# A front reordered around a two-taps-a-product convolution, and one relu over two units, in a convolution with two mixture layers

## The chip, the core and the metric

The kernel runs on one core of one Trainium2 chip. The metric is the device time of one execution in microseconds (us); the median of several executions is compared. Five engines work side by side, each through its own queue of instructions: PE (TensorE, matrix products), ACT (ScalarE), DVE (VectorE), POOL (GpSimd) and SP (which here only issues DMAs).

## The reference

```python
def _attn_ref(x, weight):            # x: 2 x 4096 x 192, weight: 8 heads x 7 taps
    w = softmax(weight)              # over the 7 taps, with 1e-9 in the divisor
    out[t] = sum over k of w[head, k] * x_pad[t + k]      # causal, head by head of channels

def _moe_ref(x, w_in, w_out):        # x: 8192 x 192, w_in: 192 x 2048, w_out: 2048 x 192
    h = x @ w_in
    g = where(h >= 1, h, where(h <= -1, 0, (h + 1)**2 / 4))
    return g @ w_out

def _moe2_ref(x, w_in, w_out):
    h = x @ w_in
    return (h * sigmoid(1.702 * h)) @ w_out

# the result is _moe2_ref(_moe_ref(_attn_ref(x)))
```

## The kernel before, in words

The 8192 tokens are cut into 16 blocks of T = 512. The 192 channels are cut into an "a" part of 128 (one block to a tile) and a "b" part of 64 (two blocks to a tile). For each block the kernel makes the convolution and then two layers, numbered 1 (the clipped square) and 2 (the sigmoid product). Each value of x, of the weights and of the gate is split into a high and a low part (`xah`, `xal`; `ghi`, `glo`), and a product is made from three products of the parts.

**Units and steps.** A unit is one slice of 128 hidden channels of one layer and one block; there are 16 units for each of 32 phases (a phase is a layer and a block), 512 in all. The main loop takes two units a step. `both(u, v)` puts on PE the first product of units u, u+1 (into one of two `pair` tiles of two banks each, which alternate from step to step) and the second product of units u-4, u-3 (into the two `acc` banks of a phase). The products have 64 rows, and PE is given them in couples, the low half of the rows beside the high half, 19 couples a step. The `pair` tile is complete with the 15th couple.

**Gates.** `gates(u)` turns the two banks of a `pair` tile into `ghi` and `glo`. For layer 1: ACT makes relu((h+1)/2) into tile `a` (line 319) and its square (line 320), DVE takes the bound max(h, 1) and the smaller of it and the square (line 326), ACT makes the high part (line 330), DVE the low part (line 334). Three forms exist. In the first two phases (`units[u][0] < B`, with the conversions of weights in between, the "fill" below) relu and square run over both units at once. In the later layer 1 phases the four operations `early(0), bound(0), early(1), bound(1)` run unit by unit; these are 14 phases of 8 steps, 112 steps. In layer 2 it is one activation a unit (line 322), its high and its low part.

**Order.** Everything is written in program order inside `manual_schedule`; each engine takes its own instructions in that order and waits on semaphores. Beside the gates some steps hold other work, placed by `at(unit, op)`: the convolution of later blocks on DVE (lines 185, 186, two taps a step, some of them in layer 1 steps), its parts (lines 79, 80), the end of a phase (`finish`, lines 465 to 492). The weights come as 64 bit words through SP; `convert_at` sets the steps at which each tile of weights (two units of one layer) is loaded, scaled (ACT), shifted and joined (DVE), and split into high and low (line 155 on ACT or DVE, lines 160 and 165 on DVE).

**The front.** Before the loop: taps and x are loaded, PE runs two products on constants (`warm_up`), DVE and ACT make the exponentials of the taps, ACT makes seven diagonals of 128 by 128 for the b part of both blocks, POOL six for the a part of block 1. PE convolves the b part in quarters of its array (line 215, seven taps), DVE the a part of block 0 (lines 185, 186), and PE six taps of the a part of block 1 with 128 by 128 diagonals (line 204), two taps before the first products of units 0, 1 (`first_only(0)`) and four behind them; ACT makes the seventh tap (line 220). Then come `first_only(2)` and, as step 2, the first `both`. Step n below is the one with units 2n and 2n+1.

Of the kernel before, what the change touches and what calls it, by code (L numbers as in the profile page):

```python
# [8 lines left out]
F32 = mybir.dt.float32  # L9
# [6 lines left out]
P = 128  # L16
# [4 lines left out]
def kernel(  # L21
# [46 lines left out]
    def bank(n, name):  # L68
        return ps.tile([P, T], F32, tag=f"bank{n}", name=name)
# [5 lines left out]
    def f32(ap):  # L75
        return ap.bitcast(F32)
# [12 lines left out]
    def exponentials():  # L89
        mx = const.tile([P, 2], F32, name="mx")  # L90
        nc.vector.tensor_reduce(mx, taps, axis=AX.X, op=ALU.max)
        nc.vector.tensor_sub(taps, taps, mx.unsqueeze(2).to_broadcast([P, 2, K]))
        nc.scalar.activation(exps, taps, AF.Exp)

    def softmax_taps():
        return [
            lambda: nc.vector.tensor_reduce(share, exps, axis=AX.X, op=ALU.add),
            lambda: nc.vector.tensor_scalar_add(share, share, 1e-9),
            lambda: nc.vector.reciprocal(share, share),
            lambda: nc.vector.tensor_mul(taps, exps, share.unsqueeze(2).to_broadcast([P, 2, K])),  # L100
        ]


    words = {1: w1, 2: w2}
# [67 lines left out]
    def new_xs():  # L172
        return [xs_p.tile([P, T], F32R, tag=t, name=t) for t in ("xah", "xal", "xbh", "xbl")]

    def x_load(part, i, queue=None):

        t = xt_p.tile([P, T + 128], F32, tag=f"xt{part}", name="xt", bufs=2 - part)[:, 0 : PAD + T]
        (queue or nc.sync).dma_start(t, (xb if part else xa)[i])
        return t
# [7 lines left out]

        return [tap(k) for k in range(K)]

    def warm_up(w):  # L190
# [6 lines left out]
    def diagonals(part, eng_mul, d):  # L197
        for k in range(len(d)):
            eng_mul(d[k], ident, exps[:, part, k : k + 1])

    def conv_on_pe(t, c, d):

        def tap(k):
            return lambda: nc.tensor.matmul(c, d[k], t[:, k : k + T], start=False, stop=k == len(d) - 1)  # L204

        return [tap(k) for k in range(len(d))]

    def conv_by_quarters(t, cs, d):

# [6 lines left out]

        return [lambda k=k: tap(k) for k in range(K)]

    def first_tap(part, t, c, k):
        nc.scalar.mul(c, t[:, k : k + T], exps[:, part, k : k + 1])  # L220

    def high_of_sum(part, hi, c):
        nc.scalar.mul(hi, c, share[:, part : part + 1])
# [87 lines left out]
    def gate_ops(u):  # L311

        n, _ = phases[units[u][0]]
        h = hid.pop(u)
        a = a_p.tile([P, 2, T], F32, tag="a", name="a")

        def early(k=slice(0, 2)):
            if n == 1:
                nc.scalar.activation(a[:, k], h[:, k], AF.Relu, bias=0.5, scale=0.5)  # L319
                nc.scalar.activation(a[:, k], a[:, k], AF.Square)  # L320
            else:
                nc.scalar.activation(a[:, k], h[:, k], AF.Gelu_apprx_sigmoid)  # L322
# [12 lines left out]

        return early, bound, high, low

    def gates(u, conversions=()):
        early, bound, high, low = gate_ops(u)
        if units[u][0] < B:  # L340
            early()
            for op in conversions:
# [163 lines left out]


    def gates_beside_finish(u, p, conversions):
        early, bound, high, low = gate_ops(u)
        up, down, add, bh, bl, ah, al = finish_ops(p)  # L510
        ops = [early, up, ah, down, *conversions, lambda: bound(0), lambda: bound(1), al, add]
# [31 lines left out]
    def fetch_x(*which):  # L543
        for part, i in which:
            xt[part, i] = x_load(part, i)
# [11 lines left out]
    with tc.manual_schedule():  # L557
        first, second = halves_of
        nc.sync.dma_start(taps, taps_in)
        xt[1, 0] = x_load(1, 0, nc.scalar)  # L560
        xt[0, 0] = x_load(0, 0)
        xt[0, 1] = x_load(0, 1, nc.scalar)
        fetch_w(1, 0, first)
        fetch_w(1, 1, first)
        fetch_w(1, 0, second)
        fetch_w(1, 1, second)
# [4 lines left out]
        exponentials()  # L571
# [6 lines left out]
        shares = softmax_taps()  # L578
        db = o_p.tile([P, K, P], F32, tag="o", name="diag")
        db = [db[:, k] for k in range(K)]  # L580
        da = [f32(t).rearrange("p (k c) -> p k c", c=P) for t in new_xs()]
        da = [da[k // 4][:, k % 4] for k in range(K - 1)]
        diagonals(1, nc.scalar.mul, db)
        diagonals(0, nc.gpsimd.tensor_scalar_mul, da)
        b_ops = conv_by_quarters(xt[1, 0], cb_ps, db)
        a1 = conv_on_pe(xt[0, 1], ca_ps, da)
# [15 lines left out]
        steps += ((5, 7, 8, 9, 9, 10), (6, 8, 10, 11, 11, 12), (8, 10, 12, 13, 13, 14), (9, 11, 14, 15, 15, 16))  # L602
# [9 lines left out]
        def of(ops, step):  # L612
            return ops.get(step, [])

        w0, w1_ = parts_of(0), parts_of(1)
        run(*b_ops)
        run(lambda: nc.scalar.activation(table, ident[:, 0:1], AF.Gelu_apprx_sigmoid))
        run(*a0[0:5], *shares, *w0[0][0:2], lambda: first_tap(0, xt[0, 1], ca_ps, K - 1), *w0[0][2:4])
        run(*a0[5:], *w0[0][4:], w1_[0][0], *put_sum(0, 0), *w1_[0][1:3], *put_sum(0, 1), *w1_[0][3:])
        straight, crossed, last, closing = first_only(0)  # L620
        run(*a1[0:2], straight, last, lambda: crossed(closing), *a1[2:])
        run(*of(fetches, 0))
        run(*w0[1], *put_sum(1, 1), *w1_[1][0:3])
        early, bound, high, low = gate_ops(0)
        run(*of(act, 0))
        early()
        run(*of(dve, 0))
        bound(0)
        run(*put_sum(1, 0))
        bound(1)  # L630
        for k in (0, 1):
            high(k)
            low(k)
        run(*w1_[1][3:])
        straight, crossed, last, closing = first_only(2)
        run(straight, last, lambda: crossed(closing))
        run(*of(fetches, 1), *of(dve, 1))
        gates(2, of(act, 1))

        def beside(step):  # L640
            for op in plan.get(step, []):
# [77 lines left out]
```

## Time and profile before

| what | value |
|---|---|
| runs | 1179.79, 1181.0, 1181.41 us; median 1181.0 |
| the profiled execution's own time | 1180.55 us |
| its span (first to last instruction) | 1178.8 us |
| PE matmul, busy | 1150.7 us |
| PE weight load, busy | 924.6 us |
| ACT, busy | 841.1 us |
| DVE, busy | 718.0 us |
| POOL, busy | 5.5 us |
| DMA, mean | 26 GB/s |

An execution takes 1.75 us more than its span here. Busy time counts the stretches in which at least one instruction of the engine was running. A row of a timeline is: start, duration, engine, line, operation, tiles, shape, and in brackets the idle time of the engine ahead of it with what ended it; a count xN at the end says that N equal instructions that follow each other are merged.

### The profile page before, as it was taken

To read this page: it belongs to the slowest core of one execution; us is meant where nothing else is said; L and a number is where in the kernel's file an instruction comes from. 1 tells how busy PE (TensorE), PEld (TensorE's weight loads), DVE (VectorE), ACT (ScalarE), POOL (GpSimd) and SP (SyncE) were. 2 spreads that over 40 slices of the span, in tenths; PEclk is the share of its full clock that TensorE was granted. 3 is DMA by queue.
4 is the path that set the end of the run, shared out by engine and by line. 5 is a ranking of instruction groups with operands and counts; after the bars stand their busy time and mean duration, and the time that the engine had idled before them with its cause. 6 is when DMAs were issued, how large, how long until landed. Compare 5 with 4: busy or idle time off the path is not lost.

```text
span 1178.8 us, 23909 instructions
## 1 busy us (share of the span) xinstructions
PE 1150.7 (98%) x9780; PEld 924.6 (78%) x9780; DVE 718.0 (61%) x1099; ACT 841.1 (71%) x1420; POOL 5.5 (0%) x12
## 2 busy tenths in 40 slices
PE   9999999999999999999999999999999999999998
PEld 4999986677786877868778787787878778787786
DVE  7997756675646756466574655646556475564533
ACT  7998677776767677676776667767677676776754
POOL 1000000000000000000000000000000000000000
PEclk9999999999999999999999999999999999999999
DMA  6442011000100001000010000100001000000000
GB/s 187 120 119 60 1 44 30 1 10 14 28 11 14 11 14 28 11 14 10 15 37 1 15 10 15 37 13 3 10 15 37 15 1 10 14 11 14 2 1 28
DMA packets 23756, 30.44 MB, mean 26 GB/s; under 512 B 3296, under 2 KB 15840, under 8 KB 23648
## 3 DMA queue, kind: packets, MB, share of 16 engines
q1 hardware_dynamic: 23216, 28.27, 8.4%
q8 instruction: 77, 1.26, 0.4%
q10 hardware_dynamic: 432, 0.66, 0.2%
q14 instruction: 31, 0.25, 0.1%
HBM read 18.96 MB, written 6.29 MB: 21 GB/s over the span
## 4 chain that ended last, share of the span: by engine, by line
PE 66%; ACT 20%; DVE 11%; issue 3%; DMA 0%; ACTq 0%; DVEq 0%
PE acc L417 33%; PE pair L417 31%; DVE a L326 10%; ACT a L320 8%; ACT a L319 7%; ACT ghi L330 3%; DVE glo L334 1%; PE cb_ps L215 1%; ACT o L488 1%; DVE cva L186 1%; ACT o L492 0%; PE ca_ps L204 0%; PE acc L391 0%; DMA taps<-in_taps_dram 0%; DVE cva L185 0%
## 5 line engine op out<-in xcount | busy, mean ns | idle before, releaser
L417 PE MATMUL acc<-ghi,wt 64*128 64x512 f32 x3048 | 666.9, 388 | 0.0
L417 PE MATMUL acc<-glo,wt 64*128 64x512 f32 x2032 | 574.2, 389 | 0.0
L417 PEld LDWEIGHTS acc<-ghi,wt 64*128 64x128 f32 x3048 | 465.1, 184 | 54.3
L334 DVE TENSOR_TENSOR glo<-a,ghi 128x512 fp32r<-128x512 f32 x512 | 351.1, 689 | 203.6 <-ACT ghi L330 185.6
L417 PE MATMUL pair<-xah,wt 64*128 64x512 f32 x2048 | 444.5, 397 | 22.4 <-DVE a L326 22.3
L417 PEld LDWEIGHTS acc<-glo,wt 64*128 64x128 f32 x2032 | 329.2, 184 | 51.1 <-DVE glo L334 18.2
L330 ACT CAST ghi<-a 128x512 fp32r<-128x512 f32 x512 | 315.7, 618 | 45.7 <-DVE a L326 35.5
L417 PEld LDWEIGHTS pair<-xah,wt 64*128 64x128 f32 x2048 | 278.8, 184 | 85.0 <-DVE a L326 56.2
L326 DVE SCALAR_TENSOR_TENSOR a<-pair,a 128x512 f32<-128x512 f32 x256 | 175.5, 690 | 229.2 <-ACT a L320 229.2
L417 PE MATMUL pair<-xal,wt 64*128 64x512 f32 x1024 | 298.6, 387 | 0.0
L417 PE MATMUL pair<-xbh,wt 64*128 64x512 f32 x1024 | 274.5, 387 | 0.0
L322 ACT ACTIVATE a<-pair 128x512 f32<-128x512 f32 x256 | 152.1, 594 | 124.1 <-PE pair L417 124.1
L319 ACT ACTIVATE a<-pair 128x512 f32<-128x512 f32 (+1 forms) x240 | 150.0, 625 | 121.4 <-DVE a L326 96.0
L417 PEld LDWEIGHTS pair<-xbh,wt 64*128 64x128 f32 x1024 | 187.8, 184 | 18.5
L417 PE MATMUL pair<-xbl,wt 64*128 64x512 f32 x512 | 197.3, 387 | 0.0
L320 ACT ACTIVATE a<-a 128x512 f32<-128x512 f32 (+1 forms) x240 | 158.6, 661 | 7.6
L417 PEld LDWEIGHTS pair<-xal,wt 64*128 64x128 f32 x1024 | 142.9, 184 | 18.8
L417 PEld LDWEIGHTS pair<-xbl,wt 64*128 64x128 f32 x512 | 93.9, 184 | 9.0
L186 DVE SCALAR_TENSOR_TENSOR cva<-xt,taps,cva 128x512 f32<-128x512 f32 x84 | 62.9, 749 | 1.5
L186 DVE SCALAR_TENSOR_TENSOR cvb<-xt,taps,cvb 128x512 f32<-128x512 f32 x42 | 31.5, 749 | 0.7
L79 ACT CAST xah<-cva 128x512 fp32r<-128x512 f32 x14 | 8.7, 619 | 12.1 <-DVE cva L186 12.1
L149 DVE SCALAR_TENSOR_TENSOR wd<-wa,wd 128x768 uint32<-128x768 uint32 (+2 forms) x18 | 15.6, 867 | 0.8
(64 smaller groups left out, 249.3 us busy)
## 6 DMA issues: line engine op xcount, KB each, us to landing
raw<-in_w_dram SPq DMA_DIRECT2D x48, 128.0 KB, 2.3
xt<-in_xa_dram SPq DMA_DIRECT2D x15, 259.0 KB, 3.0
out_dram<-o SPq DMA_DIRECT2D x15, 256.0 KB, 2.0
raw<-in_w_dram SPq DMA_DIRECT2D x48, 64.0 KB, 2.4
raw<-in_w_dram SPq DMA_DIRECT2D x16, 192.0 KB, 2.7
out_dram<-o SPq DMA_DIRECT2D x17, 128.0 KB, 2.3
xt<-in_xb_dram SPq DMA_DIRECT2D x7, 259.0 KB, 3.1
xbh<-xbh SPq DMA_DIRECT2D x14, 128.0 KB, 2.2
```

Source lines behind the costliest of these rows:

```text
L79: nc.scalar.copy(hi, src)
L149: nc.vector.scalar_tensor_tensor(d(), a().bitcast(U32), 3, d(), op0=ALU.logical_shift_left, op1=ALU.bitwise_or)
L186: return lambda: nc.vector.scalar_tensor_tensor(c, x, w, c, op0=ALU.mult, op1=ALU.add)
L215: nc.tensor.matmul(c[o], d[k][r, r], t[r, k : k + T], start=k == 0, stop=k == K - 1)
L319: nc.scalar.activation(a[:, k], h[:, k], AF.Relu, bias=0.5, scale=0.5)
L320: nc.scalar.activation(a[:, k], a[:, k], AF.Square)
L322: nc.scalar.activation(a[:, k], h[:, k], AF.Gelu_apprx_sigmoid)
L326: nc.vector.scalar_tensor_tensor(a[:, k], h[:, k], 1.0, a[:, k], op0=ALU.max, op1=ALU.min)
L330: nc.scalar.copy(halves[u + k][0], a[:, k])
L334: nc.vector.tensor_sub(lo, a[:, k], f32(hi))
L417: mm = nc.tensor.matmul(banks[n], w, r, start=n in fresh, stop=ends.get(n) == k)
L488: nc.scalar.copy(o[0:DB, 1], acc_b[DB:P])
```

## The change

Layer 1's gates of the later phases: one relu over both units, one square for each, then the two bounds. In the front: the a part of block 1 is loaded twice, as two tiles of 128 rows; each holds 64 channels as they are and the same 64 channels one token later, so that a product with a 128 by 64 matrix of two diagonals makes two taps for 64 channels; the two sides go to the two column halves of PE's array. Three such couples make six taps, and ACT makes the seventh in two operations of 64 rows. For the exponentials in that layout PE makes four products of 7 columns and ACT a copy. The products on constants become 512 and 128 columns ahead and 448 behind these. The x loads of block 0 and of the b part both go through SP, the two new loads through ACT behind the diagonals. The order of the front's conversions and sums is new, gates 0 and 2 take two squares, and the steps of the first tiles of weights move (`steps`).

```diff
-    const.tile([P, 40], F32, name="pad")
+    twice = const.tile([P, H], F32, name="twice")
+    exps_s = const.tile([P, 2, K], F32, name="exps_s")
+    const.tile([P, 88], F32, name="pad")
...
+    def shifted(src, first, shift, *rest):
+        return bass.AP(tensor=src.tensor, offset=src.offset + first, ap=[[shift, 2], *rest])
...
-        for k, n in enumerate((T, T // 2)):
-            nc.tensor.matmul(w[:, 0:n], ones, wide[:, 0:n], start=k == 0, stop=False)
+        for k, n in enumerate(sizes):
+            nc.tensor.matmul(w[:, 0:n], ones, wide[:, 0:n], start=fresh and k == 0, stop=False)
+
+    def spread_exps(t):
+        flat = exps.rearrange("p i k -> p (i k)")
+        for j in (0, 1):
+            for s in (0, 1):
+                rows = slice(s * H, s * H + H)
+                nc.tensor.matmul(t[rows, j], ident[:, j * H : j * H + H], flat[:, s : s + K], start=True, stop=True)
...
+    def double_diagonals(d):
+        nc.gpsimd.tensor_add(twice, ident[:, 0:H], ident[:, H:P])
+        for m in range(K // 2):
+            for j in (0, 1):
+                nc.gpsimd.tensor_scalar_mul(d[j][m], twice, exps_s[:, j, 2 * m : 2 * m + 1])
...
-            return lambda: nc.tensor.matmul(c, d[k], t[:, k : k + T], start=False, stop=k == len(d) - 1)
+        def pair_of_taps(m):
+            for j, side in enumerate(sides):
+                x = ts[j][:, 2 * m : 2 * m + T]
+                nc.tensor.matmul(c[side], d[j][m], x, start=False, stop=m == K // 2 - 1)
...
             if n == 1:
                 nc.scalar.activation(a[:, k], h[:, k], AF.Relu, bias=0.5, scale=0.5)
-                nc.scalar.activation(a[:, k], a[:, k], AF.Square)
...
+        def square(k=slice(0, 2)):
+            nc.scalar.activation(a[:, k], a[:, k], AF.Square)
...
         elif phases[units[u][0]][0] == 1:
+            early()
+            square(0)
+            square(1)
             for k in (0, 1):
-                early(k)
                 bound(k)
...
-        xt[1, 0] = x_load(1, 0, nc.scalar)
-        xt[0, 0] = x_load(0, 0)
-        xt[0, 1] = x_load(0, 1, nc.scalar)
+        fetch_x((0, 0), (1, 0))
...
-        warm_up(ca_ps)
+        warm_up(ca_ps, (T, T // 4), True)
...
+        spread_exps(es_ps)
+        warm_up(ca_ps, (7 * T // 8,), False)
...
-        steps = ((0, 0, 0, 1, 2, 2), (0, 1, 1, 3, 3, 4), (1, 2, 3, 4, 5, 5), (2, 4, 6, 6, 6, 7), (3, 5, 7, 8, 8, 9))
+        steps = ((0, 1, 1, 1, 2, 2), (0, 2, 2, 3, 4, 5), (1, 3, 3, 4, 4, 6), (2, 5, 5, 6, 6, 7), (3, 7, 7, 8, 8, 9))
...
-        run(*a1[0:2], straight, last, lambda: crossed(closing), *a1[2:])
+        run(a1[0], straight, last, lambda: crossed(closing), *a1[1:])
...
```

In a row of `steps` the numbers are the steps of load, scale, shift, join, high part and low part; the first row is the tile of units 4 and 5 of a phase, the second that of units 6 and 7, which step 6 is the first to use.

ACT in a layer 1 step of the later phases, before (names: `pair` the sums, `a` the gate, `acc` and `o` the end of an earlier phase; in brackets whose semaphore the instruction waits for):

```order
L319 ACTIVATE a<-pair_2270 128x512 [waits PE_49]
L320 ACTIVATE a<-a 128x512 [waits Activation_49]
L319 ACTIVATE a<-pair_2270 128x512 [waits DVE_49]
L320 ACTIVATE a<-a 128x512 [waits Activation_49]
L330 CAST ghi<-a 128x512 [waits PE_49]
L330 CAST ghi<-a 128x512 [waits DVE_49,PE_49]
```

The same step now:

```order
L346 ACTIVATE a<-pair_2284 128x1024 [waits PE_49]
L351 ACTIVATE a<-a 128x512 [waits Activation_49]
L351 ACTIVATE a<-a 128x512
L359 CAST ghi<-a 128x512 [waits DVE_49,PE_49] x2
L520 COPY o<-acc_3_1645 64x512 [waits DMAHW3_49,DMAHW2_49,PE_49]
```

The relu no longer stands twice, and no relu waits for DVE within the step; both casts now do. On DVE the step has two bounds and two low parts as before, and each bound has a wait of its own on ACT:

```order
L355 SCALAR_TENSOR_TENSOR a<-pair_2284,a 128x512 [waits PE_49,Activation_49]
L355 SCALAR_TENSOR_TENSOR a<-pair_2284,a 128x512 [waits Activation_49]
L363 TENSOR_TENSOR glo<-a,ghi 128x512 [waits PE_49,Activation_49] x2
L191 SCALAR_TENSOR_TENSOR cva<-xt,taps,cva 128x512
L191 SCALAR_TENSOR_TENSOR cva<-xt,taps,cva 128x512 [waits DVE_49]
```

DVE in the fill, steps 3 and 4, before (`pair_408` is step 3's, `pair_476` step 4's; lines 160 and 165 are the low part of the weights that step 6 is the first to use):

```order
L326 SCALAR_TENSOR_TENSOR a<-pair_408,a 128x512 x2
L334 TENSOR_TENSOR glo<-a,ghi 128x512 x2
L160 TENSOR_TENSOR wt_90<-wd,wt_90 128x640
L165 TENSOR_TENSOR wt_90<-wd,wt_90 128x2x64
L149 SCALAR_TENSOR_TENSOR wd<-wa,wd 128x768
L326 SCALAR_TENSOR_TENSOR a<-pair_476,a 128x512 x2
L334 TENSOR_TENSOR glo<-a,ghi 128x512 x2
```

And now (`pair_420` is step 3's, `pair_490` step 4's; lines 165 and 170 are the same low part):

```order
L355 SCALAR_TENSOR_TENSOR a<-pair_420,a 128x512 x2
L363 TENSOR_TENSOR glo<-a,ghi 128x512 x2
L154 SCALAR_TENSOR_TENSOR wd<-wa,wd 128x768
L160 CAST wt_92<-wd 128x768
L355 SCALAR_TENSOR_TENSOR a<-pair_490,a 128x512 x2
L363 TENSOR_TENSOR glo<-a,ghi 128x512 x2
L165 TENSOR_TENSOR wt_92<-wd,wt_92 128x640
L170 TENSOR_TENSOR wt_92<-wd,wt_92 128x2x64
```

The low part has moved from ahead of step 4's bounds to behind step 4's low parts of the gate.

PE at the start of the front now (before it began with 512 and 256 columns of line 195, and `cb_ps` followed at once):

```order
L200 MATMUL ca_ps<-const-float32-1.0 128x512
L200 MATMUL ca_ps<-const-float32-1.0 128x128
L207 MATMUL es_ps<-exps,ident 64x7 x4
L200 MATMUL ca_ps<-const-float32-1.0 128x448
L237 MATMUL cb_ps_117<-xt,diag 64x512 x2
L237 MATMUL cb_ps_118<-xt,diag 64x512 x2
```

Four small products that need the exponentials, and 448 columns on constants, now stand between those exponentials and the convolution of the b part.

## Rows read from the trace of the kernel before

**Rows 1.** The page: busy us by engine, and PE's granted clock in 40 slices.

```profile
PE 1150.7 (98%) x9780; PEld 924.6 (78%) x9780; DVE 718.0 (61%) x1099; ACT 841.1 (71%) x1420; POOL 5.5 (0%) x12
...
PEclk9999999999999999999999999999999999999999
```

**Rows 2.** Timeline of PE: the first four products of a step, seven steps.

```profile
23.82 0.62 PE L417 MATMUL pair<-xah,wt 64*128 64x512 f32 x4
...
41.09 0.64 PE L417 MATMUL pair<-xah,wt 64*128 64x512 f32 x4
...
101.52 0.66 PE L417 MATMUL pair<-xah,wt 64*128 64x512 f32 x4
...
144.59 0.66 PE L417 MATMUL pair<-xah,wt 64*128 64x512 f32 x4
...
202.38 0.73 PE L417 MATMUL pair<-xah,wt 64*128 64x512 f32 x4
207.00 0.73 PE L417 MATMUL pair<-xah,wt 64*128 64x512 f32 x4
...
1165.47 0.62 PE L417 MATMUL pair<-xah,wt 64*128 64x512 f32 x4
```

**Rows 3.** Timeline of ACT, one layer 1 step of the later phases.

```profile
202.94 0.59 ACT L319 ACTIVATE a<-pair 128x512 f32<-128x512 f32 x1
203.57 0.63 ACT L320 ACTIVATE a<-a 128x512 f32<-128x512 f32 x1
204.96 0.60 ACT L319 ACTIVATE a<-pair 128x512 f32<-128x512 f32 x1 [0.76 <-DVE a L326]
205.59 0.63 ACT L320 ACTIVATE a<-a 128x512 f32<-128x512 f32 x1
206.13 0.60 ACT L330 CAST ghi<-a 128x512 fp32r<-128x512 f32 x1
207.04 0.62 ACT L330 CAST ghi<-a 128x512 fp32r<-128x512 f32 x1 [0.30 <-DVE a L326]
```

**Rows 4.** Timeline of DVE: the two bounds of that step.

```profile
204.24 0.69 DVE L326 SCALAR_TENSOR_TENSOR a<-pair,a 128x512 f32<-128x512 f32 x1 [0.47 <-ACT a L320]
206.26 0.69 DVE L326 SCALAR_TENSOR_TENSOR a<-pair,a 128x512 f32<-128x512 f32 x1 [1.33 <-ACT a L320]
```

**Rows 5.** Waits of the whole span (us in total, times, longest): relu behind bound.

```profile
ACT a L319 <- DVE a L326: 96.0, 112, 1.8
```

**Rows 6.** Groups by line and shape: prices (busy us, mean ns).

```profile
L319 ACT ACTIVATE a<-pair 128x1024 f32<-128x1024 f32 x16 | 16.3, 1020 | 0.1
...
L488 ACT COPY o<-acc 64x512 f32<-64x512 f32 x16 | 9.4, 584 | 3.0 <-PE acc L391 2.6
...
L186 DVE SCALAR_TENSOR_TENSOR cva<-xt,taps,cva 128x512 f32<-128x512 f32 x84 | 62.9, 749 | 1.5
...
L160 DVE TENSOR_TENSOR wt<-wd,wt 128x640 fp32r<-128x640 f32 x14 | 11.5, 820 | 0.1
```

**Rows 7.** Timeline of PE, the front: constants, quarters of the b part, taps.

```profile
0.76 2.90 PE L195 MATMUL ca_ps<-const-float32-1.0 128*128 128x512 f32 x4 [0.76 <-PEq L705]
...
4.48 8.70 PE L215 MATMUL cb_ps<-xt,diag 64*64 64x512 f32 x56 [0.83 <-ACT diag L199]
...
17.66 1.98 PE L204 MATMUL ca_ps<-xt,xah 128*128 128x512 f32 x4
```

**Rows 8.** Timeline of PE's weight loads in those quarters, two loads a tap.

```profile
7.10 0.25 PEld L215 LDWEIGHTS cb_ps<-xt,diag 64*64 64x64 f32 x4 [0.60 <-issue]
7.95 0.25 PEld L215 LDWEIGHTS cb_ps<-xt,diag 64*64 64x64 f32 x4 [0.61 <-issue]
...
10.02 0.14 PEld L215 LDWEIGHTS cb_ps<-xt,diag 64*64 64x64 f32 x4 [0.29 <-issue]
10.44 0.14 PEld L215 LDWEIGHTS cb_ps<-xt,diag 64*64 64x64 f32 x4 [0.29 <-issue]
```

**Rows 9.** Timeline of DVE in the fill: the low parts of step 4.

```profile
40.69 1.30 DVE L334 TENSOR_TENSOR glo<-a,ghi 128x512 fp32r<-128x512 f32 x2
```

More of the change, by code (lines that the diff above doesn't have):

```diff
@@ L188, in conv_taps, with warm_up, diagonals, conv_by_sides @@
         return [tap(k) for k in range(K)]
-    def warm_up(w):
+    def warm_up(w, sizes, fresh):
         ones = nc.const_aps.tensor(1.0, [P, P], F32)
         wide = nc.const_aps.tensor(1.0, [P, T], F32)
-        for k, n in enumerate((T, T // 2)):
-            nc.tensor.matmul(w[:, 0:n], ones, wide[:, 0:n], start=k == 0, stop=False)
[L197 to L203, printed above, removed]
-            return lambda: nc.tensor.matmul(c, d[k], t[:, k : k + T], start=False, stop=k == len(d) - 1)
-        return [tap(k) for k in range(len(d))]
+        for k, n in enumerate(sizes):
[6 more added lines that the diff above has]
+                nc.tensor.matmul(t[rows, j], ident[:, j * H : j * H + H], flat[:, s : s + K], start=True, stop=True)
+    def diagonals(part, d, begin=0):
+        for k in range(begin, len(d)):
+            nc.scalar.mul(d[k], ident, exps[:, part, k : k + 1])
+    def double_diagonals(d):
[3 more added lines that the diff above has]
+                nc.gpsimd.tensor_scalar_mul(d[j][m], twice, exps_s[:, j, 2 * m : 2 * m + 1])
+    def conv_by_sides(ts, c, d):
+        sides = slice(0, H), slice(H, P)
+        def pair_of_taps(m):
+            for j, side in enumerate(sides):
+                x = ts[j][:, 2 * m : 2 * m + T]
+                nc.tensor.matmul(c[side], d[j][m], x, start=False, stop=m == K // 2 - 1)
+        return [lambda m=m: pair_of_taps(m) for m in range(K // 2)]
     def conv_by_quarters(t, cs, d):
@@ L217, in conv_by_quarters, with last_tap, of_side @@
         return [lambda k=k: tap(k) for k in range(K)]
-    def first_tap(part, t, c, k):
-        nc.scalar.mul(c, t[:, k : k + T], exps[:, part, k : k + 1])
+    def last_tap(ts, c):
+        def of_side(j):
+            x = ts[j][0:H, PAD : PAD + T]
+            nc.scalar.mul(c[j * H : j * H + H], x, exps_s[0:H, j, K - 1 : K])
+        return [lambda: of_side(0), lambda: of_side(1)]
     def high_of_sum(part, hi, c):
@@ L334, in low @@
             nc.vector.tensor_sub(lo, a[:, k], f32(hi))
-        return early, bound, high, low
+        return early, square, bound, high, low
     def gates(u, conversions=()):
-        early, bound, high, low = gate_ops(u)
+        early, square, bound, high, low = gate_ops(u)
         if units[u][0] < B:
             early()
+            square()
             for op in conversions:
@@ L508, in gates_beside_finish @@
     def gates_beside_finish(u, p, conversions):
-        early, bound, high, low = gate_ops(u)
+        early, square, bound, high, low = gate_ops(u)
         up, down, add, bh, bl, ah, al = finish_ops(p)
-        ops = [early, up, ah, down, *conversions, lambda: bound(0), lambda: bound(1), al, add]
+        ops = [early, square, up, ah, down, *conversions, lambda: bound(0), lambda: bound(1), al, add]
         ops += [lambda: high(0), lambda: high(1), bh, lambda: low(0), lambda: low(1), bl]
@@ L559 @@
         nc.sync.dma_start(taps, taps_in)
-        xt[1, 0] = x_load(1, 0, nc.scalar)
-        xt[0, 0] = x_load(0, 0)
-        xt[0, 1] = x_load(0, 1, nc.scalar)
[L563 to L566, printed above, removed]
+        fetch_x((0, 0), (1, 0))
+        for g in (0, 1):
+            fetch_w(1, g, first)
+        for g in (0, 1):
+            fetch_w(1, g, second)
         cb_ps, ca_ps = [bank(k, f"cb_ps{k}") for k in (3, 1)], bank(2, "ca_ps")
-        warm_up(ca_ps)
+        warm_up(ca_ps, (T, T // 4), True)
         make_identity(nc, ident)
-        exponentials()
+        less_max(taps)
+        nc.scalar.activation(exps, taps, AF.Exp)
+        es_ps = bank(0, "es_ps")[:, 0 : 2 * K].rearrange("p (j k) -> p j k", k=K)
+        spread_exps(es_ps)
+        warm_up(ca_ps, (7 * T // 8,), False)
         table = const.tile([P, 1], F32, name="table")
@@ L577 @@
         a0 = conv_taps(0, xt[0, 0], ca, exps)
-        shares = softmax_taps()
         db = o_p.tile([P, K, P], F32, tag="o", name="diag")
         db = [db[:, k] for k in range(K)]
[L581 to L584, printed above, removed]
+        diagonals(1, db[0:2])
+        nc.scalar.copy(exps_s, es_ps)
+        diagonals(1, db, 2)
+        da = [f32(t).rearrange("p (k c) -> p k c", c=H) for t in new_xs()[0:2]]
+        da = [[d[:, m] for m in range(K // 2)] for d in da]
+        double_diagonals(da)
+        wide = a_p.tile([P, 2, T], F32, tag="a", name="xt1").rearrange("p k t -> p (k t)")
+        pair_x = [xt_p.tile([P, T + 128], F32, tag="xt0", name="xt"), wide]
+        pair_x = [t[:, 0 : PAD + T] for t in pair_x]
+        for j, t in enumerate(pair_x):
+            nc.scalar.dma_start(t, shifted(xa[1, j * H : (j + 1) * H], 0, 1, [PAD + T, H], [1, PAD + T]))
         b_ops = conv_by_quarters(xt[1, 0], cb_ps, db)
-        a1 = conv_on_pe(xt[0, 1], ca_ps, da)
+        a1 = conv_by_sides(pair_x, ca_ps, da)
+        tap6 = last_tap(pair_x, ca_ps)
         def run(*ops):
@@ L613, in of @@
             return ops.get(step, [])
-        w0, w1_ = parts_of(0), parts_of(1)
+        (sc0, sh0, jo0, hi0, *lo0), (sc0o, sh0o, jo0o, hi0o, *lo0o) = parts_of(0)
+        (sc1, sh1, jo1, hi1, *lo1), (sc1o, sh1o, jo1o, hi1o, *lo1o) = parts_of(1)
+        (a0h, a0l), (b0h, b0l), (b1h, b1l), (a1h, a1l) = (put_sum(*k) for k in ((0, 0), (0, 1), (1, 1), (1, 0)))
         run(*b_ops)
         run(lambda: nc.scalar.activation(table, ident[:, 0:1], AF.Gelu_apprx_sigmoid))
-        run(*a0[0:5], *shares, *w0[0][0:2], lambda: first_tap(0, xt[0, 1], ca_ps, K - 1), *w0[0][2:4])
-        run(*a0[5:], *w0[0][4:], w1_[0][0], *put_sum(0, 0), *w1_[0][1:3], *put_sum(0, 1), *w1_[0][3:])
+        run(*a0[0:5], softmax_taps, sc0, sh0, jo0, hi0, *tap6, *a0[5:], sc1, *lo0, sh1, a0h, a0l, jo1, b0h, b0l)
         straight, crossed, last, closing = first_only(0)
-        run(*a1[0:2], straight, last, lambda: crossed(closing), *a1[2:])
[L622 to L634, printed above, removed]
+        run(a1[0], straight, last, lambda: crossed(closing), *a1[1:])
+        run(hi1, sc0o, sc1o, sh0o, jo0o, *lo1, hi0o, sh1o, b1h, jo1o, *lo0o, b1l)
+        early, square, bound, high, low = gate_ops(0)
+        run(early, lambda: square(0), lambda: square(1), lambda: bound(0), lambda: bound(1))
+        run(*of(fetches, 0), a1h, a1l, lambda: high(0), lambda: high(1), lambda: low(0), lambda: low(1), hi1o, *lo1o)
         straight, crossed, last, closing = first_only(2)
         run(straight, last, lambda: crossed(closing))
-        run(*of(fetches, 1), *of(dve, 1))
-        gates(2, of(act, 1))
+        early, square, bound, high, low = gate_ops(2)
+        scale, (shift, join) = of(act, 1), of(dve, 1)
+        run(*of(fetches, 1), early, lambda: square(0), lambda: square(1), shift, *scale, lambda: bound(0))
+        run(lambda: bound(1), join, *(lambda f=f, k=k: f(k) for f in (high, low) for k in (0, 1)))
         def beside(step):
```

21 lines of the change are left out of this document (10 added, 11 removed).

## The prediction

> **What bounds the kernel now.** I read the page first: PE is busy 98% of the span [rows 1], so it looks as if at most 1178.8 - 1150.7 = 28.1 us could be won. Then I read the timeline of PE at the places where a step begins [rows 2]. From 101.52 to 144.59, in the first two phases, ten steps take 43.07, 4.307 us each, 0.227 for each of the 19 couples; there PE goes without a gap and sets the pace. A layer 1 step of the later phases takes 207.00 - 202.38 = 4.62 with the same 38 products. From the first `both` at 23.82 to the last at 1165.47 there are 253 steps in 1141.65 us. At 4.307 they would be 1089.7, so **52.0 us are lost to steps that are too long**.
>
> This is more than the idle time of PE, and the two readings must be weighed. In the row, idle time is what no product covers, and one product is longer than the distance to the next couple, so late products close part of a gap in the books [rows 1, 2]. The Trainium skill, Perfetto Trace Analysis, Identifying the Most-Contended Engine, says that busy time of matmuls is no good measure of how near to the limit a kernel is, since they are pipelined, and wants the busy share of weight loads instead. Here that share is 78%, so the trace agrees, and by this rule 28.1 is no ceiling; by the busy share it would be one, and the time about 1152. I go by the distances of steps.
>
> Third, why is the step 4.62? The timeline of ACT [rows 3] with that of DVE [rows 4] reads as a zigzag. Relu and square of unit 0 end at 204.20. DVE's bound of unit 0 runs from 204.24 to 204.93. The relu of unit 1 starts at 204.96, after 0.76 idle, though its sums are there. The bound of unit 1 ends at 206.95, and the last cast starts at 207.04 after another 0.30 idle. So ACT has 3.67 us of work (0.59 + 0.63 + 0.60 + 0.63 + 0.60 + 0.62) and about 1.0 of waiting for DVE in every step. The summary of waits confirms it: the relu waited for the bound 112 times, 96.0 us [rows 5], once for each step of those 14 phases. PE is late because its `pair` banks are late; ACT and DVE sit in turn.
>
> **The gates.** The change takes that wait out. Two relus of 0.60 become one of 1.02 [rows 6]; the squares stay 0.63 each. Counted from the start of the relu: square 0 from 1.04 to 1.67, square 1 to 2.30; bound 0 waits only for square 0 (each bound has its own wait in the order), 1.70 to 2.39, bound 1 to 3.08; the casts 2.42 to 3.04 and 3.11 to 3.73. ACT's round is 3.73, **0.58 under PE's 4.307**, where it was 0.3 over. The one relu starts when both banks are closed, with the 15th couple, 15 x 0.227 = 3.4 us into the step; the bounds free the banks 3.1 later, at 6.5 to 6.7. PE needs them two steps after their start, at 8.61, so 1.9 us are left. Some steps hold one more copy on ACT, 0.584 [rows 6]: 4.31, just the pace. Some hold two taps on DVE, 2 x 0.749 [rows 6], beside two bounds of 0.69 [rows 4] and two low parts that take 1.30 [rows 9], 4.2 in all. Where a step holds more, for a step or two, the 1.9 us cover it. So I let all steps run at PE's pace: **-52.0**. What is late next is PE itself.
>
> Layer 2 steps and the fill change nothing in their gates. That a step at PE's pace is not quite free is seen in the fill: 28 steps from 23.82 to 144.59 took 120.77, 0.17 over 28 x 4.307 [rows 2]. Scaled to 225 more steps I hold back **+1.4**.
>
> **The front, convolution.** The a part of block 1 takes six taps of PE before. Four records, two taps, take 1.98, by their starts 0.91 each [rows 7], 5.5 us in all. Now it is three couples. If the two column halves run side by side, as the four quarters of line 215 do (eight records a tap), a couple costs 0.91, 2.7 in all; if one after the other, 5.5 again. The quarters are the nearest row: **-2.8**, bound 0.
>
> The start moves the other way. The convolution of the b part began at 4.48 [rows 7], just behind the first diagonal. Now four small products and 448 columns on constants stand between. 768 columns took 2.90 [rows 7], 448 take 1.7, the small ones perhaps 0.5 (between 0.1 and 1.0), from about 4.0 on: start at 6.2, 1.7 late. The rate matters as much: half a tap took 0.85 at 7.10 and 0.42 at 10.02 [rows 8], the ratio of PE's two levels, 1.2 and 2.4 GHz, though the page's granted clock is at 9 in all slices [rows 1]. Between 4.48 and the rise PE had worked without a pause for some 5.1 us. If the rise stays at 9.6, 3.4 us of the new convolution run slow, two taps of 1.7, and five of 0.85 follow: end at 13.9 instead of 13.18, +0.7. If it comes 5.1 after 4.0, +0.4; if 5.1 after 6.2, +1.6. I take **+0.7**.
>
> The x loads move from ACT's queue to SP's, where the b part's is third and ahead of all weights, and the second pair of loads, each as large as the one it replaces, stands behind the diagonals on ACT. They are wanted behind the b part's convolution, some 6 us later; the cover is that convolution. The weights come about half a microsecond later, and ACT scales the first of them behind its two load issues. POOL's six diagonals are half as wide and have the same cover. The sums of block 0 come later too, since ACT makes the seventh tap in two pieces first; their cover is the first couple of taps on PE. All these at zero; if the cover fails, a microsecond.
>
> **The front, steps.** One move has a price. Step 6 is the first to use the second tile of weights that the loop converts, and its low part now stands behind step 4's low parts of the gate on DVE. Before, those ran from 40.69 to 41.99 [rows 9], and step 6 began at 41.09, its second couple at 41.32 [rows 2]. With 0.75 more of 0.820 behind the 41.99 [rows 6] it comes at 42.7, and PE waits **+1.4** (0 if ACT and DVE are by then so much further ahead of PE than before, 2 if they lag more; the two squares of gates 0 and 2 and ACT's scalings let me expect a lag, and I add 0.4 for a late `pair` at step 4). With -2.8 + 0.7 + 1.8 the front comes to **-0.3**.
>
> **The sum.** The profiled execution's own time is 1180.55, the span and 1.75 around it. 1180.55 - 52.0 + 1.4 - 0.3 = 1129.65. The median of the runs shown is 0.45 above that execution, so about **1130**. The tail behind 1165.47 is untouched.
>
> **The rivals.** *PE's pace is reached only in part* (9%). If bound 0 waited for both squares, bound 0 ended at 3.03, the casts at 3.7 and 4.3: ACT's round is the pace itself, and each of 14 phases keeps what its extra copies and taps take, 1.2 to 2 us, 22 in all: about 1152, by chance what the busy share gives. For it speaks that some tracker made the relu wait for a bound of the other bank; against it, the separate waits of the two bounds in the order.
>
> *The front loses* (8%). The rise of PE's clock waits for the new convolution and comes late, or the second tile of weights is later still: +4 to +8, 1134 to 1138. The Trainium skill, TensorE: Matmul & The Clock Gate, Part 1, has the array start at the lower level and rise by activity; the rows agree, and they do not tell how much of a pause it bears.
>
> *Slower* (2%). The merged gate becomes one chain: relu 1.04, both squares 1.26, both bounds 1.4, both casts 1.24, with hand-overs about 5.0. Its place is the layer 1 step, and it decides as soon as that chain is longer than the 4.62 of now and the next relu waits for its end. Price: 5.0 - 4.62 = 0.38 in 112 steps, +43 on 1180: 1222. Against it: the fill has the same form with a relu of 1024 [rows 6], and its steps are at 4.307 [rows 2].
>
> *It doesn't do what it says* (1%). The relu then waits for the bounds of the step before, which ended before the last cast: nothing lost and nothing won against my sum unless the wait is as long as now; then 1180.
>
> **How the numbers follow.** My forecast holds 80%, with its own range from 1126 (no stall at step 6, clock rising early) to 1135 (clock late, twice the residue). The range reaches up to the second rival and a little past it, 1125 to 1140; left out are the first and the last two, 12%. A measurement of this kernel can tell 0.2% from no change, 2.4 us. Faster by more: all but the last two, 0.97; same 0.01; slower 0.02.
>
> **What would show it.** Right: the row "relu behind bound" is gone from the waits; layer 1 steps are 4.31 apart; ACT's idle time in them ends with PE; the last `both` starts some 1090 to 1093 after the first; step 2 starts near 22, and step 6 about 1.4 late behind a DVE low part. Wrong: layer 1 steps stay over 4.4, or DVE or ACT waits show up in them each time; the b part's convolution ends after 15.

## The result and the profile after

| what | before | after |
|---|---|---|
| median of 4 executions | 1180.66 us | 1142.45 us (1141.74 to 1143.39) |
| ratio, 95% interval | 1 | 0.9677 (0.966 to 0.9694) |
| the profiled execution's own time, its span | 1180.55, 1178.8 | 1141.74, 1139.9 |

38.2 us were won where 1180.66 - 1130.0 = 50.7 were forecast; the time lies 2.45 us above the range. (The kernel before has one more execution here, 1180.33 us, than when the prediction was made, hence the other median.) The books of the two profiled executions can be closed with three numbers, all from starts of `both` on PE.

Timeline of PE after, first products of a step: step 2, step 5, step 7, steps 15 and 31 (161.96 - 92.92 = 69.04 us for these sixteen), the last.

```profile
35.25 0.62 PE L449 MATMUL pair<-xah,wt 64*128 64x512 f32 x4
...
48.45 0.64 PE L449 MATMUL pair<-xah,wt 64*128 64x512 f32 x4
...
58.47 0.62 PE L449 MATMUL pair<-xah,wt 64*128 64x512 f32 x4
...
92.92 0.62 PE L449 MATMUL pair<-xah,wt 64*128 64x512 f32 x4
...
161.96 0.66 PE L449 MATMUL pair<-xah,wt 64*128 64x512 f32 x4
...
1126.65 0.66 PE L449 MATMUL pair<-xah,wt 64*128 64x512 f32 x4
```

- First to last `both`: 1126.65 - 35.25 = 1091.40, before 1141.65 [rows 2]: **-50.25**. From 161.96 to 1126.65 there are 224 steps in 964.69 us, 4.307 each, in both layers.
- Start of step 2: 35.25, before 23.82 [rows 2]: **+11.43**.
- The rest of the span behind the last `both`: 13.25 and 13.33.

Page after: busy us by engine, and PE's granted clock in 40 slices.

```profile
PE 1120.0 (98%) x9790; PEld 1095.8 (96%) x9790; DVE 710.5 (62%) x1098; ACT 831.0 (73%) x1312; POOL 5.3 (0%) x14
...
PEclk7999999999999999999999999999999999999999
```

Against [rows 1] PE's busy share stands at 98% as before, while the weight loads went from 78% to 96%: that the kernel is 38 us shorter shows in the second figure alone. The waits of the whole span after (us in total, times, longest) no longer have a row of a relu behind a bound [rows 5]; relu and bound wait mostly for PE now.

```profile
DVE a L355 <- PE acc L449: 123.1, 73, 2.9
ACT a L346 <- PE pair L449: 64.7, 84, 1.9
```

So everything behind step 7 is as forecast, and the loss lies in the front. Timeline of PE there, after (what stands at 4.48 and 17.66 in [rows 7]):

```profile
3.24 0.60 PE L207 MATMUL es_ps<-exps,ident 128*64 128x7 f32 x8
3.77 1.69 PE L200 MATMUL ca_ps<-const-float32-1.0 128*128 128x448 f32 x2
5.39 6.24 PE L237 MATMUL cb_ps<-xt,diag 64*64 64x512 f32 x56
25.62 1.09 PE L226 MATMUL ca_ps<-xt,xah 128*64 128x512 f32 x1 [13.99 <-ACT ca_ps L245]
```

The b part's convolution ends at 11.63, then PE does nothing for **13.99 us**, until ACT has made the seventh tap. Timeline of ACT after in that time:

```profile
8.11 1.70 ACTq L624 DMA_DIRECT2D xt<-in_xa_dram  x2
9.85 1.28 ACT L660 ACT_TABLE_LOAD   x1 [4.33 <-DMA xt<-in_xa_dram]
...
11.25 0.59 ACT L148 ACTIVATE wa<-raw 128x448 f32<-128x448 f32 x1
...
18.76 0.69 ACT L245 ACTIVATE ca_ps<-xt,exps_s 64x512 f32<-64x512 f32 x1 [5.66 <-DMA xt<-in_xa_dram]
24.83 0.69 ACT L245 ACTIVATE ca_ps<-xt,exps_s 64x512 f32<-64x512 f32 x1 [5.39 <-DMA xt<-in_xa_dram]
```

ACT waits three times for something about the second pair of x loads: 4.33 us around their issue, 5.66 for the first to land, 5.39 for the second. The sums of block 0, which the first couple of layer 1 needs, all stand on ACT behind these two taps. The chain of waits after, from 0 to 40 us (start, us, what), says the same:

```profile
5.88 2.21 DMA raw<-in_w_dram
8.09 0.02 issue
8.11 1.14 ACTq L624
9.25 0.04 issue
9.29 15.46 DMA xt<-in_xa_dram
```

The second load is on its way from 9.29 on and takes **15.46 us** for 259 KB; the three x loads of the same size in the front of the kernel before landed in 2.8 to 3.8 us, and that of block 0, from SP, takes 2.6 after. Also, the issue at 8.11 was released by a load of weights that landed at 8.09. The view of the DMAs after, from 19 to 24 us (mean busy share of 16 engines in tenths, GB/s, share by queue), shows how slow the loads are when nearly nothing else moves:

```profile
DMA packets 134, 0.25 MB, mean 50 GB/s; under 512 B 4, under 2 KB 32, under 8 KB 134
...
q10 hardware_dynamic: 102, 0.21, 11.0%
q1 hardware_dynamic: 32, 0.04, 2.0%
```

50 GB/s at 13% of 16 engines: about two engines are at work (q10 is ACT's queue with the two new loads, 0.21 of the 0.25 MB). In the new loads' source pattern, `[[1, 2], [518, 64], [1, 518]]`, the outermost dimension is 2.

### The profile page after: what moved, and what is told of

The parts are those of the page before. It is cut to its first block, busy times and chain, and to the rows that moved or that the text cites. A ratio compares the mean times of both kernels' runs of the same rounds, so it can differ in the third digit from the quotient of the medians.

```text
span 1139.9 us, 23934 instructions
## 1 busy us (share of the span) xinstructions
PE 1120.0 (98%) x9790; PEld 1095.8 (96%) x9790; DVE 710.5 (62%) x1098; ACT 831.0 (73%) x1312; POOL 5.3 (0%) x14
## 4 chain that ended last, share of the span: by engine, by line
PE 97%; DMA 2%; SPq 0%; DVE 0%; ACT 0%; issue 0%; ACTq 0%; DVEq 0%
PE acc L449 50%; PE pair L449 46%; DMA xt<-in_xa_dram 1%; PE acc L423 0%; PE ca_ps L226 0%; SPq L128 0%; DMA raw<-in_w_dram 0%; ACT ghi L359 0%; ACTq L624 0%; DVE wd L154 0%; SPq L183 0%; DVE wt L165 0%; DVE glo L363 0%; ACT ca_ps L245 0%; DVE a L355 0%
## 5 line engine op out<-in xcount | busy, mean ns | idle before, releaser
L449 PE MATMUL acc<-ghi,wt 64*128 64x512 f32 x3048 | 678.0, 387 | 0.0
L449 PE MATMUL acc<-glo,wt 64*128 64x512 f32 x2032 | 586.4, 386 | 0.0
L449 PEld LDWEIGHTS acc<-ghi,wt 64*128 64x128 f32 x3048 | 488.8, 184 | 3.2
L363 DVE TENSOR_TENSOR glo<-a,ghi 128x512 fp32r<-128x512 f32 x512 | 342.7, 691 | 224.5 <-ACT ghi L359 206.3
L449 PEld LDWEIGHTS acc<-glo,wt 64*128 64x128 f32 x2032 | 338.1, 184 | 2.4
L449 PEld LDWEIGHTS pair<-xah,wt 64*128 64x128 f32 x2048 | 302.9, 185 | 7.6 <-ACT xbh L250 1.6
L355 DVE SCALAR_TENSOR_TENSOR a<-pair,a 128x512 f32<-128x512 f32 x256 | 164.9, 686 | 164.5 <-PE acc L449 123.1
L346 ACT ACTIVATE a<-pair 128x1024 f32<-128x1024 f32 x128 | 131.6, 1028 | 66.3 <-PE pair L449 64.7
L449 PEld LDWEIGHTS pair<-xal,wt 64*128 64x128 f32 x1024 | 151.9, 185 | 1.3
L351 ACT ACTIVATE a<-a 128x512 f32<-128x512 f32 (+1 forms) x242 | 146.4, 649 | 4.1
```

The costliest lines, as they stand in the source:

```text
L449: mm = nc.tensor.matmul(banks[n], w, r, start=n in fresh, stop=ends.get(n) == k)
```

## The experiments

**Which part of the load is slow.** Theory A: the outermost dimension of 2 keeps a load on two engines. B: the loads are issued too late. C: source rows that overlap or start one number off are slow to read. Three kernels vary one thing each.

e1_split makes each load two of 64 rows:

```diff
-            nc.scalar.dma_start(t, shifted(xa[1, j * H : (j + 1) * H], 0, 1, [PAD + T, H], [1, PAD + T]))
+            for s in (0, 1):
+                x = xa[1, j * H : (j + 1) * H]
+                x = bass.AP(tensor=x.tensor, offset=x.offset + s, ap=[[PAD + T, H], [1, PAD + T]])
+                nc.scalar.dma_start(t[s * H : s * H + H], x)
```

> The changed kernel, with each of the second pair's two loads issued as two of 64 rows (132.6 KB each, the upper rows' source one number further on), from the same place on ScalarE; nothing else. Theory A, the outermost dimension of 2 keeps each load on 2 of the 16 DMA engines (50 GB/s at a DMA share of 0.11 from 18 to 24 us): the four loads land in 2.5 to 4 us each, the 14.0 us of TensorE idle before the a part's convolution fall under 2 us, step 2 starts near 22 us rather than 35.25, and the run takes 1128 to 1132 us. Theory B, late issue on ScalarE's queue behind the slot waits: two more issues of about 0.5 to 1 us make it later still, 1142 to 1144. Theory C, the shifted or overlapping source rows are slow to read: the upper halves stay slow, 1138 to 1143. By what the Trainium skill's page DMA: Bandwidth & Descriptors says in its section on why a DMA adds 16 to its semaphore (a copy runs on the largest number up to 16 that divides the slowest dimension of both sides) it would be A.

Measured: 1135.14 us, ratio to before 0.9616 (0.9601 to 0.963). The loads land in 3.1 to 4.4 us, shifted halves and all, PE's idle time in front of the taps falls from 14.0 to 4.3. C falls, A holds, but only 7.3 us came back, about half of what A alone expected. The timelines of PE and of ACT in e1_split show what is left:

```profile
18.22 1.09 PE L226 MATMUL ca_ps<-xt,xah 128*64 128x512 f32 x1 [4.29 <-ACT ca_ps L245]
...
8.09 5.33 ACTq L627 DMA_DIRECT2D xt<-in_xa_dram  x4
13.45 1.28 ACT L663 ACT_TABLE_LOAD   x1 [7.83 <-DMA xt<-in_xa_dram]
...
14.85 0.58 ACT L148 ACTIVATE wa<-raw 128x448 f32<-128x448 f32 x1
```

Four issues of about half a microsecond each, some 2.1 us together, are spread over 5.33 us, and ACT is held from 5.6 to 13.4: the scale of the first weight tile (line 148) starts at 14.85. So B has a part too, in a form that I had not thought of: an issue can wait.

e2_apart keeps the outermost dimension of 2, without overlap or odd shift:

```diff
-            nc.scalar.dma_start(t, shifted(xa[1, j * H : (j + 1) * H], 0, 1, [PAD + T, H], [1, PAD + T]))
+            nc.scalar.dma_start(t, shifted(xa[1, j * H : (j + 1) * H], 0, P * (PAD + T), [PAD + T, H], [1, PAD + T]))
```

> The changed kernel with the same two loads, an outermost dimension of 2 and 64 rows in each half, but the second half is read from the next tile's rows (128 x 518 numbers further on) in place of the same rows one number further on: no overlap and no odd shift. Part of block 1's first convolution is computed from other data. Theory A (outermost dimension of 2): still about 50 GB/s, landing at 18 to 25 us, 14 us of TensorE idle, 1141 to 1144 us. Theory C (overlap or the one-number shift): the loads land in 2.5 to 4 us, 1128 to 1132 us. Theory B (late issue): unchanged, 1141 to 1144.

Measured: 1142.68 us, 0.9681 (0.9667 to 0.9696), the time of the changed kernel. Busy time by stretch in e2_apart (the last two numbers are DMA share and GB/s):

```profile
15.00:20.00 5.00, 0.00 (x0) 0.00 (x0) 0.00 (x0) 0.15 (x1) 0.00 (x0) 0.59 0.37 118
20.00:25.00 5.00, 0.00 (x0) 0.00 (x0) 0.00 (x0) 0.54 (x1) 0.00 (x0) 0.50 0.13 49
```

Again two engines and 49 GB/s. What the rows hold does not matter; with e1_split, the dimension is shown to be the cause of the slow landing. The Trainium skill, DMA: Bandwidth & Descriptors, has this rule in its section on why a DMA increments its semaphore by 16: a copy runs on the largest number of engines, at most 16, that divides the slowest dimension of both sides, so an outermost 2 leaves two. The trace agrees, with 2.1 of 16 (13%) here.

e3_early has the loads as they are, but issues them first on ACT (the lines that make `wide` and `pair_x` and the two `dma_start` stand behind `fetch_x`).

> The changed kernel with the two loads as they are, but issued first on ScalarE, ahead of the exponentials and the diagonals, in place of behind the diagonals. Theory A: 518 KB at about 50 GB/s still take 10.5 us or more from 1 to 2 us on, so the last lands at 13 to 18 us (the weight tiles share those two engines), the idle time falls to 3 to 7 us and the run takes 1131 to 1137 us. Theory B (late issue alone is to blame): each lands in 2.5 to 4 us, no idle time is left, 1127 to 1131 us.

Measured: 1138.01 us, 0.9641 (0.9627 to 0.9655), 1 us above what A allowed. The chain of waits in e3_early says why:

```profile
0.71 1.15 ACTq L597
1.86 0.03 issue
1.89 16.03 DMA xt<-in_xa_dram
17.92 0.02 issue
17.94 0.47 SPq L128
...
19.09 2.14 DMA raw<-in_w_dram
...
21.34 0.61 ACT wa L148
```

The second load is still under way for 16.03 us, and when it lands at 17.92, an issue of weights on **SP** goes out at 17.94: SP had been waiting for it, though the two have no tile in common. The waits of SP's queue in e3_early, for loads of x:

```profile
SPq L128 <- DMA xt<-in_xa_dram: 12.3, 3, 5.4
```

In the changed kernel it was ACT that waited for a load that SP had issued (landed at 8.09, issue at 8.11, above). So an issue can be held by an earlier DMA of another queue. The reason stands in the program as it is built from these kernels: the DMAs of both queues take eight completion counters in turn, in program order, and from the ninth DMA on nearly every issue first waits until the DMA eight places before it, which used the same counter, has landed. In e3_early the slow second load is the fifth DMA, and the issue at 17.94 is the thirteenth; in the changed kernel ACT's first new load is the nineteenth, and the eleventh is the load of weights that lands at 8.09.

**Both together.** e6_split_early is e3_early with the split loads of e1_split.

> The changed kernel with the second pair's loads split into four of 64 rows and issued first on ScalarE, ahead of the exponentials. What e1_split and e3_early left apart is put together. Theory: the front's loss has two causes, the outermost dimension of 2 (50 GB/s) and ScalarE held from 5.6 to 13.4 us in its own issues, which wait for the completion of earlier loads that SyncE has issued; with both gone ScalarE reaches the first weight tile's scale at 8 to 9 us as in the kernel before, the first couple starts at 12 to 16 us, step 2 at 21 to 24 us, and the run takes 1126 to 1130.5 us. Rival: the new front itself is slower whatever the loads do (its chain through ScalarE and VectorE): 1132 us or more, step 2 behind 26 us.

Measured: 1129.08 us, 0.9569 (0.9555 to 0.9583). Timelines of ACT (the first scale) and of PE (step 2) in e6_split_early:

```profile
9.80 0.61 ACT L148 ACTIVATE wa<-raw 128x448 f32<-128x448 f32 x1 [1.13 <-DMA raw<-in_w_dram]
...
23.53 0.62 PE L449 MATMUL pair<-xah,wt 64*128 64x512 f32 x4
```

The scale comes later than the 8 to 9 us that the theory gave it, step 2 and the time are within its bounds. The front's loss is gone with these two causes; the rival falls.

e8_by_sync tells ACT's hold from the late landing: e1_split with `nc.sync.dma_start` in place of `nc.scalar.dma_start`, at the same place of the program.

> e1_split with its four loads of 64 rows issued at the same place of the program, but on SyncE's queue behind the first fourteen weight loads, so that ScalarE holds no issue. Theory: in e1_split ScalarE was held from 5.6 to 13.4 us by its own issues, and the first weight tile's scale came at 14.85 rather than 7.4; now ScalarE goes on at 5.6, the loads land near 13 to 15 us, the last tap follows, and step 2 starts at 24 to 27 us: 1129.5 to 1133 us, between e1_split (1135.1) and e6_split_early (1129.1). Rival: only the landing of the loads counts, not ScalarE's hold; they land no sooner than in e1_split, so 1134 to 1136 us.

Measured: 1131.2 us, 0.9586 (0.9573 to 0.96), as the theory had it. The scale starts at 6.87, and ACT now waits for the first of the loads, at the seventh tap:

```profile
6.87 0.62 ACT L148 ACTIVATE wa<-raw 128x448 f32<-128x448 f32 x1
...
13.47 0.69 ACT L245 ACTIVATE ca_ps<-xt,exps_s 64x512 f32<-64x512 f32 x1 [3.18 <-DMA xt<-in_xa_dram]
```

So of the 13.4 us between the changed kernel and e6_split_early, 7.3 are the two engines and 3.9 ACT held in its own issues. The remaining 2.1 stand between e8_by_sync and e6_split_early, whose loads come early; here PE waits 3.14 us for the seventh tap, and then takes 2.93 us for unit 0's products (1.72 in e6_split_early). These prices hold in this order of the steps: e3_early, which moves the loads without splitting them, gains 4.4.

**Is the gain the gates' alone, and is it the wait or the merged relu?** e4_gates is the kernel before with the new gates only; e5_order is the kernel before with its own relus and squares, and the bounds behind all four.

```diff
             for k in (0, 1):
                 early(k)
+            for k in (0, 1):
                 bound(k)
```

> The kernel before with one edit: layer 1's relu of a couple is one instruction of 1024 columns, then the two squares, then the two bounds; front, steps and loads as before. My theory: all 52 us of the gain are this edit's, so 1128 to 1130 us, layer 1's steps 4.31 us apart, step 2 still at 23.8 us; the new front by itself has lost about 13. Rival: part of the 4.31 us pace comes from the new steps or the new front, so this edit alone leaves 1135 us or more.

Measured: 1128.27 us, 0.9559 (0.9543 to 0.9575).

> The kernel before, with layer 1's gates only put in another order: relu and square of the first unit, relu and square of the second, then the two bounds; the relus stay two instructions of 512 columns each. If the gain lies in taking the bound out from between the two relus (my theory), this alone reaches the 4.31 us pace: 1127 to 1131 us. If it needs the one relu of 1024 columns (its saved fixed time on ScalarE), a good part of the 52 us stays: 1140 to 1181 us.

Measured: 1128.1 us, 0.9559 (0.9543 to 0.9575). Timeline of PE in e5_order, the first and the last `both`:

```profile
22.73 0.73 PE L418 MATMUL pair<-xah,wt 64*128 64x512 f32 x4
...
1112.77 0.62 PE L418 MATMUL pair<-xah,wt 64*128 64x512 f32 x4
```

That is 1090.04 us for 253 steps, 4.308 each, and in e4_gates it is 1089.82. Both kernels beat the change by 14 us. The merged relu is worth nothing that can be seen; taking the bound out from between the two relus is the whole gain. In the waits of e5_order the relu waits for PE instead:

```profile
ACT a L319 <- PE pair L418: 39.9, 72, 1.9
ACT a L319 <- PE acc L418: 13.5, 7, 1.9
ACT ghi L330 <- DVE a L326: 4.3, 18, 0.7
```

**Step 6.** After, steps 5 and 7 stand 58.47 - 48.45 = 10.02 apart, 1.41 more than two steps. The waits after, from 44 to 60 us:

```profile
PEld pair L449 <- DVE wt L165: 1.5, 1, 1.5
PE pair L449 <- DVE wt L165: 1.1, 1, 1.1
```

e7_steps is e6_split_early with `(0, 2, 2, 3, 3, 4)` for `(0, 2, 2, 3, 4, 5)`.

> e6_split_early with one row of the table of steps changed: the second weight tile's high and low part one step earlier, (0, 2, 2, 3, 3, 4) in place of (0, 2, 2, 3, 4, 5). Theory: step 6 waits 1.4 us for that low part, which stands on VectorE behind step 4's last low half; moved ahead of step 4's bounds it is ready in time, so this is 1.2 to 1.7 us below e6_split_early, and the starts of steps 5 and 7 stand 8.6 us apart rather than 10.0. Rival: the 1.1 us on VectorE then delays step 4's bounds and low halves, so step 6 waits as long for those: within 0.4 us of e6_split_early.

Measured: 1129.16 us, 0.9568 (0.9554 to 0.9582): no change, the rival was right. The distance falls to 9.68 only. In e9_mixed, which has the same steps, step 6 waits for a high half of the gate on ACT, and ACT before that 1.88 us for a bound, which stands behind the conversions on DVE:

```profile
39.54 1.22 ACT L359 CAST ghi<-a 128x512 fp32r<-128x512 f32 x2 [1.88 <-DVE a L355]
```

Two more kernels look for a better version. e9_mixed is e7_steps with two of the four loads sent through SP:

```diff
-                nc.scalar.dma_start(t[s * H : s * H + H], x)
+                (nc.scalar, nc.sync)[j].dma_start(t[s * H : s * H + H], x)
```

> A version to beat the others: e7_steps with the first two of the four loads on ScalarE and the other two on SyncE between the two x loads and the weights, so that the exponentials are held by 1.2 us less and the weights come 0.9 us later. Theory: in e6_split_early the exponentials came at 4.53 rather than 2.88 us behind the four issues, and the chain runs from them through the b part's convolution to the first couple; with them earlier, step 2 starts 0.5 to 1.2 us earlier: 1127.6 to 1128.9 us. Rival: the first weight tile, 0.9 us later, takes the chain over, 1129 to 1130.5 us.

Measured: 1128.78 us, 0.9567 (0.9554 to 0.958), in the theory's range, but only 0.4 us below e7_steps, less than executions of either kernel differ by: not decided. Step 2 starts at 21.74 in its profiled execution, where the prediction had it, but step 6 still starts 5.25 behind step 5. e10_old_steps goes back to the steps of the kernel before in all rows but the first two.

> e9_mixed with the table of steps of the kernel before in all rows but the first two, so that a tile's low part and join stand no longer ahead of step 5's bounds on VectorE. Theory: in e9_mixed TensorE's step 6 waits about 1.1 us (its start 5.25 us behind step 5's) for step 4's or 5's halves, late behind the conversions on VectorE; with those of the kernel before, which shows all steps 4.31 apart once the relu's wait is gone, that wait goes: 1127.3 to 1128.2 us, the lowest so far. Rival: the conversions of this front need the new steps, because the second weight tiles are still being made at step 2; then a new wait takes its place, and the time is 1128.5 us or more.

Measured: 1127.88 us, 0.9555 (0.9542 to 0.9568). Timeline of PE in e10_old_steps, steps 5, 6 and 7:

```profile
35.94 0.62 PE L449 MATMUL pair<-xah,wt 64*128 64x512 f32 x4
40.24 0.62 PE L449 MATMUL pair<-xah,wt 64*128 64x512 f32 x4
44.55 0.62 PE L449 MATMUL pair<-xah,wt 64*128 64x512 f32 x4
```

4.30 and 4.31: the stall is gone, so what was left of it came from the new steps of the later tiles. With all of that mended, the new front comes to the time of the old one, 1127.88 against 1128.1 and 1128.27, whose intervals cover each other.

## Why the prediction was wrong

- **The gates, -52.0: right.** 253 steps took 1091.40 us against 253 x 4.307 = 1089.7. The reason given was right as far as the wait goes; the saved fixed time of the merged relu, which I put into ACT's round, was not needed (e5_order).
- **The residue, +1.4, and the steps, +1.8: the stall right, the residue too large.** Step 6 cost 1.41 as worked out (1.4), behind the same low part on DVE; all other steps together are 0.3 over the pace, where 1.8 had been held back (1.4, and 0.4 for step 4).
- **The convolution, -2.8: right in kind.** The column halves run side by side: in the changed kernel the two later couples stand 0.91 us apart from start to start, and in e6_split_early the three together take 1.01 + 1.87 = 2.9 us, where six taps had taken 5.5.
- **The start of the b part's convolution, +0.7: wrong way in this execution.** The small products took 0.60 (0.5 assumed), the constants 1.69 (1.7), but the taps had landed at 2.5, and it began at 5.39 instead of 6.2; and it took 6.24 us, none of it slow, and ended at 11.63 instead of 13.9. In e1_split, with the same products in front, it took 8.26 us and ended at 13.93, so the term isn't refuted. (Its upper bound, +1.6, comes to 1.5 when it is worked out again.) In the changed kernel it cost nothing either way: PE then waited 14 us.
- **The step that failed: "All these at zero; if the cover fails, a microsecond".** The second pair of loads was costed by its size, "each as large as the one it replaces", and given a cover of 6 us. But a load's time hangs on its pattern: with an outermost dimension of 2, two engines moved some 50 GB/s, the load took 15.46 us instead of the 3.8 of the one that it replaces, and its issue on ACT held the first weight tile. The cover failed by 14 us, not by one, and the step cost 13.4 us: e6_split_early, the same change with the loads split and early, takes 1129.08, where 1130.0 was forecast for the change. That it comes so near is in part luck. In its profiled execution step 2 starts at 23.53, 1.8 later than 23.82 - 2.8 + 0.7, and the 1.5 us too much held back for the steps make up for it.
- **The rivals.** *The front loses* was right in its place and wrong in its mechanism. PE's granted clock did fall, to 0.50 from 20 to 25 us, the lower level, but after PE had stood idle from 11.63 on; what ran slow afterwards (the first taps 2.06 us instead of 1.01, unit 0's couples 2.36 instead of 1.72) is 1.7 of the 13 us. So its price, 4 to 8, came out too small. *Pace reached only in part*, *slower* and *doesn't do what it says* fall with the 4.307 us steps.
- **The choice between the busy share and the distances of steps** was right: the 50.25 us gained in steps are more than the 28.1 us of PE's idle time of before, so that idle time was no ceiling.

## What to carry to other kernels

Cost a DMA by its access pattern, not by its bytes: look at the outermost dimension of both sides, and split a pattern that begins with a small number into several loads, each with many rows outermost. Look also at which engine issues it and at the load eight places before it in program order, for in a program that shares out eight completion counters like this one, an issue can hold all that stands behind it on its engine until that load, of whatever queue, has landed. And when one bundle of edits holds a large sure gain (here an order of four instructions) and a restructured front, time them apart: the first alone was the better kernel.

## What was not expected of the hardware

Two loads of 259 KB, slowed to two of 16 engines, also held back SP's loads of weights in e3_early, which use other tiles and another queue: the landing of the second one and the next issue on SP are 20 ns apart. What couples the queues is the program's turn of completion counters, told above.

The convolution of the b part, the same 56 products each time, took 6.24 us in the changed kernel and in e5_order, 6.9 in e7_steps and e8_by_sync, 7.5 in e9_mixed, 7.9 in e2_apart, 8.2 to 8.4 in e1_split, e3_early, e4_gates, e6_split_early and e10_old_steps, and 8.7 in the kernel before, and the granted clock shows 1.00 in all of these stretches. The view of that tile gives the duration of one record (ns, least, median, most), first of the changed kernel:

```profile
L237 PE MATMUL cb_ps<-xt,diag x56: 587/589/641, 5.4 to 11.0; 64*64 64x512 f32 x56
```

and of e6_split_early:

```profile
L237 PE MATMUL cb_ps<-xt,diag x56: 587/589/1109, 7.4 to 15.0; 64*64 64x512 f32 x56
```

The longest records are nearly twice as long, about the ratio of PE's two levels, 1.2 and 2.4 GHz, without a trace of it in the granted clock. They stand at the start: in e6_split_early the records up to 11.4 us take 1057 ns in the median, those behind 589. So the end of that convolution moves by up to 2 us between executions. What decides it was not tried, and neither was whether it is why the last versions, within 1.3 us of each other, can't be told apart.
